# Transposing the state's weights on VectorE in place of TensorE, with later reads and loads, in a fused attention and gated feed-forward kernel

## Chip, cores, metric

One core of one Trainium2 chip. The metric is device time in microseconds, the median of several executions. A profile comes from one execution of the kernel; that of the kernel before took 791.23 us and is not among the three timed ones in the table below. "PE" is TensorE, "DVE" VectorE, "ACT" ScalarE, "POOL" GpSimd, "SP" the engine that issues most DMAs.

## The reference, cut to what matters

```python
# x (8, 8, 512, 64), state (8, 8, 32, 64): batches, heads, tokens, width
scores  = scale * x @ state^T   ; a  = softmax(scores)  ; xread = a  @ state
scores2 = scale * state @ x^T   ; a2 = softmax(scores2) ; sread = a2 @ x
y = concat([xread, sread], axis=2) -> rows of 512        # (4352, 512)
h = y @ w_in                      # 512 -> 2048
out = (h * cos(h)) @ w_out        # 2048 -> 512
```

`a2 @ x` sums over tokens, so TensorE needs a2 with tokens on partitions. The kernel has it with the state rows on partitions (`z2`) and must transpose it: `a2T`. This transpose is what the change moves.

## The kernel before: what the change and the argument touch

```python
class Attention:                       # one for each batch b; ... cuts
    self.spread, self.z2 = xT[:, 0:2], xT[:, 2:4]
    self.a2T = xT[:, 0:2].rearrange("p j (c m) -> p j c m", c=NC)

    def tokens_turned(self, k):        # x, loaded by DMA, turned in 32x32 blocks on DVE (L298)
        blocks = self.xT[:, k].rearrange("p (g i) -> p g i", i=32)
        nc.vector.transpose(out=blocks, in_=blocks)
    def scores(self):                  # PE, L316: needs all four k of xT
        self.per_head(stT, lambda rows, k: self.xT[rows, k, :])
    def norm1(self):                   # DVE, L383: two SBUF inputs
        nc.vector.tensor_tensor(self.aT, self.z1, self.spread, op=ALU.mult)
    def turn(self, j):                 # PE, L389: four transposes of 128x128
        for c in range(NC):
            nc.tensor.transpose(out=at[j][:, P * c:P * c + P],
                                in_=self.z2[:, j, P * c:P * c + P], identity=ident)
    def turn_kept(self, j):            # ACT, L394
        nc.scalar.copy(self.a2T[:, j].rearrange("p c m -> p (c m)"), at[j])
    def reads(self, j):                # PE, L406: weights are a2T, moving operand x_b
        ...
def part(b, name, *args):              # after reads(1) the next loads of x are issued
    ...
def hidden(t):                         # PE, L469: two matmuls, h in one of 2 PSUM buffers
    ...
def gate(t):  ...                      # ACT L475, DVE L478, ACT L483 and L484, DVE L490
# one step: hidden; attention on PE (pe[s]); ACT L475, x_act[s]; DVE L478, x_dve[s];
#           ACT L483, L484; DVE L490; y_act[s], y_dve[s]; then the products of the tile
#           three steps back (L534: two or four matmuls), which sum up in PSUM banks
#           that DVE and ACT copy out (L540, L545, L547: `held`)
def plan(b):                           # which attention part of batch b+1 stands in which step
    ...
    def late(b, s):
        pairs(s[0], b, "turn", "turn_kept", 0)
        pe[s[1]].append((b, "reads", 0))
        pe[s[2]].append((b, "reads", 1))
        x_dve[s[2]].append((b, "keep"))
        if len(s) > 3:
            turned(b, s[3])
    ...
        prod(0, b, 1, *[MAIN for _ in bank])
        prod(4, b, 2, *bank)
        prod(9, b, 3, *bank)
        if b + 1 < B:
            prod(14, b + 1, 0)
            early(b + 1, (1 + (b == 1), 2 + (b == 1), 5, 6, 7, 8, 9))
            late(b + 1, (10, 11, 12, 15))
```

`early(b, s)` takes the steps of: token turns of k = 0, 1; of k = 2, 3; scores; spread and shift; the exponentials; sums; norm1. The "steps of even batches" are those while an even batch b runs.

## Time and profile before

| | before |
|---|---|
| time, median (lowest to highest), 3 runs | 791.73 us (791.41 to 792.08) |
| span of the profiled run | 789.4 us |
| PE, DVE, ACT busy | 97%, 55%, 49% |
| PE idle from 160 to 700 us | two gaps of 0.71 us |

PE at 97% says that time can be won from PE's own work; the two gaps say where it can't. The prediction below shows the lines.

### The profile page before, as it was taken

To read this page: it belongs to the slowest core of one execution; us is meant where nothing else is said; L and a number is where in the kernel's file an instruction comes from. 1 tells how busy PE (TensorE), PEld (TensorE's weight loads), DVE (VectorE), ACT (ScalarE), POOL (GpSimd) and SP (SyncE) were. 2 spreads that over 40 slices of the span, in tenths; PEclk is the share of its full clock that TensorE was granted. 3 is DMA by queue.
4 is the path that set the end of the run, shared out by engine and by line. 5 is a ranking of instruction groups with operands and counts; after the bars stand their busy time and mean duration, and the time that the engine had idled before them with its cause. 6 is when DMAs were issued, how large, how long until landed. Compare 5 with 4: busy or idle time off the path is not lost.

```text
span 789.4 us, 7555 instructions
## 1 busy us (share of the span) xinstructions
PE 767.3 (97%) x2664; PEld 340.4 (43%) x2664; DVE 431.2 (55%) x675; ACT 389.3 (49%) x626; POOL 178.7 (23%) x119
## 2 busy tenths in 40 slices
PE   8998999899999999999999999999999999999997
PEld 3442333344344344444444434434444444455554
DVE  5879887732564467744554467635553545431531
ACT  3877964644364445643473446443563445322222
POOL 3343359684000000551000000740000004610200
PEclk9999999999999999999999999999999999999999
DMA  8485461051010610150003410340100114000021
GB/s 239 160 248 179 127 140 28 0 90 18 0 27 14 107 27 14 30 104 0 15 14 54 80 27 7 53 75 0 27 1 0 27 27 117 17 0 15 14 41 40
DMA packets 161957, 43.49 MB, mean 55 GB/s; under 512 B 153920, under 2 KB 153920, under 8 KB 161920
## 3 DMA queue, kind: packets, MB, share of 16 engines
q1 hardware_dynamic: 161024, 42.49, 24.7%
q10 hardware_dynamic: 768, 0.39, 0.2%
q8 instruction: 21, 0.34, 0.2%
q0 software_dynamic: 128, 0.13, 0.1%
q14 instruction: 16, 0.13, 0.1%
HBM read 34.08 MB, written 8.91 MB: 54 GB/s over the span
## 4 chain that ended last, share of the span: by engine, by line
PE 80%; ACT 9%; DVE 8%; issue 1%; DMA 1%; POOL 1%; SPq 0%; DVEq 0%; POOLq 0%
PE o L534 44%; PE h L469 26%; PE at L316 4%; PE o L654 3%; PE at L406 2%; DVE q L478 1%; ACT q L483 1%; ACT q L484 1%; DVE g_all L490 1%; ACT s L227 1%; ACT q L475 1%; DVE xT L336 1%; ACT xT L362 1%; DVE aT L383 1%; PE o L316 1%
## 5 line engine op out<-in xcount | busy, mean ns | idle before, releaser
L469 PE MATMUL h<-aT,sw 128*128 128x512 f32 x512 | 243.2, 598 | 10.8 <-DVE g_all L490 10.2
L534 PE MATMUL o<-g_all,w_out 128*128 128x512 f32 x512 | 236.4, 598 | 1.1 <-POOL w_out L241 1.1
L496 POOL TENSOR_TENSOR g_all<-g_all 128x512 f32<-128x512 f32 x80 | 112.1, 1424 | 450.8 <-DVE g_all L490 447.2
L475 ACT ACTIVATE q<-h 128x512 f32<-128x512 f32 (+1 forms) x144 | 82.2, 571 | 261.7 <-PE h L469 261.6
L478 DVE SCALAR_TENSOR_TENSOR q<-q,h 128x512 f32<-128x512 f32 (+1 forms) x144 | 94.2, 654 | 207.3 <-ACT q L475 207.3
L534 PE MATMUL o<-g_all,s 128*128 128x512 f32 x384 | 177.3, 598 | 0.0
L490 DVE TENSOR_TENSOR g_all<-h,q 128x512 f32<-128x512 f32 (+1 forms) x144 | 94.8, 658 | 123.9 <-ACT q L484 117.7
L469 PEld LDWEIGHTS h<-aT,sw 128*128 128x128 f32 x512 | 96.8, 191 | 136.2 <-issue 110.2
L534 PEld LDWEIGHTS o<-g_all,w_out 128*128 128x128 f32 x512 | 94.0, 190 | 125.5 <-issue 118.4
L483 ACT ACTIVATE q<-q 128x512 f32<-128x512 f32 (+1 forms) x144 | 87.6, 608 | 96.3 <-DVE q L478 96.3
L534 PEld LDWEIGHTS o<-g_all,s 128*128 128x128 f32 x384 | 70.9, 190 | 91.7 <-issue 87.3
L484 ACT ACTIVATE q<-q,halfpi 128x512 f32<-128x512 f32 (+1 forms) x144 | 100.5, 698 | 4.5
L241 POOL TENSOR_TENSOR w_out<-w_out,s 128x1024 int32<-128x1024 int32 x10 | 23.9, 2389 | 79.4 <-DVE w_out L236 79.4
L496 DVE TENSOR_TENSOR g_all<-g_all 128x512 f32<-128x512 f32 x48 | 33.2, 692 | 1.6
L443 ACT COPY sw<-at 128x512 f32<-128x512 f32 x50 | 26.8, 589 | 9.0 <-PE at L316 9.0
L469 PE MATMUL h<-sT,w_in 128*128 128x256 f32 x128 | 30.2, 379 | 0.0
L654 PE MATMUL o<-w_out,g_all 128*128 128x512 f32 x64 | 29.6, 592 | 0.0
L469 PEld LDWEIGHTS h<-sT,w_in 128*128 128x128 f32 x128 | 24.3, 190 | 10.1 <-issue 6.2
L316 PE MATMUL at<-w_in,stT 64*32 64x512 f32 x400 | 27.2, 601 | 0.0
L241 POOL TENSOR_TENSOR w_in<-w_in,s 128x1024 int32<-128x1024 int32 (+1 forms) x10 | 19.7, 1966 | 32.1 <-DVE w_in L236 18.6
L540 DVE SCALAR_TENSOR_TENSOR held<-o,held 128x512 f32<-128x512 f32 x40 | 25.3, 676 | 2.3 <-PE o L534 2.3
L561 DVE STREAM_TRANSPOSE ot<-held 128x512 f32<-128x512 f32 x32 | 22.2, 692 | 0.0
(83 smaller groups left out, 443.5 us busy)
## 6 DMA issues: line engine op xcount, KB each, us to landing
out_dram<-ot SPq DMA_DIRECT2D x132, 64.0 KB, 2.0
g_all<-in_moe_w_out_dram SPq DMA_DIRECT2D x8, 1024.0 KB, 4.9
g_all<-in_moe_w_in_dram SPq DMA_DIRECT2D x6, 1024.0 KB, 5.2
xT<-in_x_dram SPq DMA_DIRECT2D x96, 64.0 KB, 2.3
x_b<-in_x_dram SPq DMA_DIRECT2D x24, 256.0 KB, 4.7
x_b<-in_x_dram SPq DMA_DIRECT2D x16, 128.0 KB, 3.9
g_all<-in_moe_w_in_dram SPq DMA_DIRECT2D x4, 512.0 KB, 6.0
x_b<-in_moe_w_out_dram SPq DMA_DIRECT2D x1, 1024.0 KB, 6.1
```

What stands on the lines that cost most here:

```text
L241: nc.gpsimd.tensor_tensor(bits, bits, e.bitcast(I32), op=ALU.add)
L316: nc.tensor.matmul(out=(to or at)[j][Ns * k:Ns * k + Ns, 0:n], lhsT=w[D * j:D * j + D, self.b, Ns * k:Ns * k + Ns], rhs=r(slice(D * j, D * ...
L443: (copy or nc.scalar.copy)(sw_of[self.b, nt][:, j, c0:c1], to[j][:, 0:c1 - c0])
L469: nc.tensor.matmul(out=t.hp, lhsT=t.lhs(i), rhs=t.rhs(i), start=(i == 0), stop=(i == t.kn - 1))
L475: nc.scalar.activation(t.q, t.hp, func=ACTF.Copy, bias=MAGIC)
L478: nc.vector.scalar_tensor_tensor(out=t.q, in0=t.q, scalar=MAGIC, in1=t.hp, op0=ALU.subtract, op1=ALU.subtract)
L483: nc.scalar.activation(t.q, t.q, func=ACTF.Abs)
L484: nc.scalar.activation(t.q, t.q, func=ACTF.Sin, bias=halfpi, scale=-TWO_PI)
L490: nc.vector.tensor_tensor(t.g, t.hp, t.q, op=ALU.mult)
L496: engine.tensor_tensor(out, a, b, op=ALU.subtract)
L534: nc.tensor.matmul(out=acc[bank][ch], lhsT=w[:, i, P * ch:P * ch + P], rhs=g.g, start=(i == 0), stop=(i == NH - 1))
L654: nc.tensor.matmul(out=acc[MAIN][i], lhsT=t.g[:, P * i:P * i + P], rhs=w_out[:, :, t.f, :], start=(t.n_th == 0), stop=(t.n_th == NF - 1))
```

## The change

Its intent: take 48 transposes off the busiest engine and give them, as 16 pieces of 32 partitions a batch, to DVE; place the pieces behind norm1 (they overwrite `spread`), so that reads of a2T and the loads that follow must come later, across the end of the batch where the next is even.

```diff
+        def turn_block(self, k, q):
+            src = self.z2.rearrange("p j (c q i) -> p q (j c) i", q=P // 32, i=32)
+            dst = self.a2T.rearrange("p j c m -> p (j c) m")
+            rows = slice(Ns * k, Ns * k + Ns)
+            nc.vector.transpose(out=dst[32 * q:32 * q + 32, :, rows],
+                                in_=src[rows, q])
 ...
+            if b < 2:
+                pairs(s[0], b, "turn", "turn_kept", 0)
 ...
+        def blocks_turned(b, to):
+            for i in range(16):
+                to[i * 5 // 16].append((b, "turn_block", i % NK, i // NK))
 ...
+            elif odd:
+                prod(0, b, 1)
+                turned(b, 1)
+            else:
+                late(b, (None, None, 0))
+                prod(2, b, 1)
+                turned(b, 3)
             prod(4, b, 2, *bank)
-            prod(9, b, 3, *bank)
-            if b + 1 < B:
-                prod(14, b + 1, 0)
-                early(b + 1, (1 + (b == 1), 2 + (b == 1), 5, 6, 7, 8, 9))
-                late(b + 1, (10, 11, 12, 15))
+            prod(9 if odd else 10, b, 3, *bank)
+            if b + 1 < B and odd:
+                prod(13, b + 1, 0)
+                early(b + 1, (2, 3, 5, 6, 7, 8, 9))
+                blocks_turned(b + 1, (x_dve[12], y_dve[12], x_dve[13],
+                                      y_dve[13], x_dve[14]))
+                pe[15].append((b + 1, "reads", 0))
+            elif b + 1 < B:
+                early(b + 1, (4, 5, 6, 7, 8, 9, 10))
+                blocks_turned(b + 1, (y_dve[10], x_dve[11], y_dve[11],
+                                      x_dve[12], y_dve[12]))
+                late(b + 1, (None, 13, 14))
+                prod(15, b + 1, 0)
```

More of the change, by code (lines that the diff above doesn't have):

```diff
@@ L395, in turn_kept @@
                            at[j])
+        def turn_block(self, k, q):
+            src = self.z2.rearrange("p j (c q i) -> p q (j c) i", q=P // 32,
+                                    i=32)
+            dst = self.a2T.rearrange("p j c m -> p (j c) m")
+            rows = slice(Ns * k, Ns * k + Ns)
+            nc.vector.transpose(out=dst[32 * q:32 * q + 32, :, rows],
+                                in_=src[rows, q])
         def reads(self, j):
@@ L781, in late @@
         def late(b, s):
-            pairs(s[0], b, "turn", "turn_kept", 0)
-            pe[s[1]].append((b, "reads", 0))
+            if b < 2:
+                pairs(s[0], b, "turn", "turn_kept", 0)
+            if s[1] is not None:
+                pe[s[1]].append((b, "reads", 0))
             pe[s[2]].append((b, "reads", 1))
@@ L804, in plan @@
         else:
+            odd = b % 2
             bank = (SIDE,) if b == 1 else ()
@@ L807, in plan @@
                 turned(1, 0)
-            prod(0, b, 1, *[MAIN for _ in bank])
-            prod(4, b, 2, *bank)
-            prod(9, b, 3, *bank)
-            if b + 1 < B:
-                prod(14, b + 1, 0)
-                early(b + 1, (1 + (b == 1), 2 + (b == 1), 5, 6, 7, 8, 9))
-                late(b + 1, (10, 11, 12, 15))
+                prod(0, b, 1, MAIN)
+            elif odd:
[5 more added lines that the diff above has]
+                turned(b, 3)
+            prod(4, b, 2, *bank)
+            prod(9 if odd else 10, b, 3, *bank)
[11 more added lines that the diff above has]
+                prod(15, b + 1, 0)
         return pe, x_act, y_act, x_dve, y_dve
```

## The prediction

> **Words.** The feed-forward part is cut in steps: each makes one tile of h (two matmuls, L469), which a gate of five instructions on ACT and DVE turns into g_all; sixteen steps make a batch, numbered 0 to 15. During batch b TensorE also does the attention of batch b+1. "Even" and "odd" mean the running batch b. There are two buffers of h, so the h of step n can't start before the last gate instruction (L490) of step n-2 has ended.
>
> **What bounds the kernel now.** I read the page first, then the groups by form, then the timelines of PE and DVE around the operations that the change touches. From the page, busy time and the chain that ended last:
>
> ```profile
> PE 767.3 (97%) x2664; PEld 340.4 (43%) x2664; DVE 431.2 (55%) x675; ACT 389.3 (49%) x626; POOL 178.7 (23%) x119
> PE 80%; ACT 9%; DVE 8%; issue 1%; DMA 1%; POOL 1%; SPq 0%; DVEq 0%; POOLq 0%
> ```
>
> TensorE is busy for 97% of the span and makes 80% of the chain. The table of stretches puts nearly all of its 22 us of idle time before 160 us and at the very end; from 160 to 700 us its timeline shows two idle gaps, 0.71 us each. So after the start, work taken off TensorE is time, except where TensorE waits anyway. The groups of the pieces that are removed, and of the nearest kin of what is added:
>
> ```profile
> L389 PE MATMUL at<-ident,xT 128*128 128x128 f32 x64 | 8.3, 273 | 0.0
> L394 ACT COPY xT<-at 128x512 f32<-128x512 f32 x16 | 9.2, 576 | 1.4 <-PE o L534 1.4
> L298 DVE STREAM_TRANSPOSE xT<-xT 128x512 f32<-128x512 f32 x24 | 16.9, 703 | 0.0
> ```
>
> 273 ns is the latency of one transpose, not its cost: the group's busy time is 8.3 us for 64. The PE timeline shows the cost; first an even batch (2), then an odd one (3), step 10 of each:
>
> ```profile
> 240.26 1.04 PE L389 MATMUL at<-ident,xT 128*128 128x128 f32 x8
> 241.13 3.60 PE L534 MATMUL o<-g_all,w_out 128*128 128x512 f32 x8
> ```
>
> ```profile
> 321.88 1.88 PE L469 MATMUL h<-aT,sw 128*128 128x512 f32 x4
> 323.59 1.04 PE L389 MATMUL at<-ident,xT 128*128 128x128 f32 x8
> 324.46 1.88 PE L534 MATMUL o<-g_all,s 128*128 128x512 f32 x4
> 327.06 1.98 PE L469 MATMUL h<-aT,sw 128*128 128x512 f32 x4 [0.71 <-DVE g_all L490]
> ```
>
> From start to start eight transposes take 0.87 us (240.26 to 241.13). In the even batch the work around them is gapless. In the odd batch TensorE, just after them, stands still 0.71 us until DVE has ended a gate. DVE there:
>
> ```profile
> 322.27 1.24 DVE L336 STREAM_TRANSPOSE xT<-i 128x1024 f32<-128x1024 f32 x1
> 323.43 0.65 DVE L478 SCALAR_TENSOR_TENSOR q<-q,h 128x512 f32<-128x512 f32 x1
> 324.00 1.80 DVE L383 TENSOR_TENSOR aT<-aT,xT 128x1024 f32<-128x1024 f32 x1
> 325.73 0.70 DVE L561 STREAM_TRANSPOSE ot<-held 128x512 f32<-128x512 f32 x1
> 326.36 0.65 DVE L490 TENSOR_TENSOR g_all<-h,q 128x512 f32<-128x512 f32 x1
> ```
>
> It runs without a gap from 320.93 to 327.01, when L490 of step 9 ends and h of step 11 starts. That queue goes back to the exponentials of step 7 on ACT (table load at 313.31, second load at 318.88); the transposes have no part in it. Batch 5 repeats it (0.71 us at 498.12), batch 1 has 0.98 us at 155.99.
>
> **What the Trainium skill says.** "TensorE: Matmul & The Clock Gate", Part 4 (PE-mode transpose): about 275 ns each within a kernel, and the result lands in PSUM, so that a copy must follow. The trace agrees: 273 ns, and L394 is that copy; but in a row they cost 109 ns each. "VectorE: DVE Perf Modes", The three transpose paths: the DVE transposes blocks of 32x32 only. This is why the change needs 16 pieces, each reading 32 partitions and writing another 32. "VectorE: DVE Perf Modes", The TRN2 errata, gives a fixed cost per instruction, so small pieces pay more per element; the trace has 703 ns for 512 elements and 1236 for 1024, that is about 170 ns fixed. "SBUF — State Buffer", SBUF: two separate sides: VectorE instructions with two SBUF inputs, or in a two-port mode, and those of GpSimd exclude each other. The trace agrees: L383 took 1.21 us at 238.29 with POOL idle and 1.80 us at 324.00 with POOL busy, while the transpose L336 took 1.23 and 1.24 us in the same places. So the pieces should not suffer from POOL.
>
> **The change, part by part.**
> (1) Removed: 6 sets of 8 transposes on PE, 0.88 us each (step 10 lasts 6.03 us in batch 2, without them it would be the usual 5.15). The three of even batches lie on the path: -2.64 us. The three of odd batches stand ahead of a wait whose end DVE sets; without them TensorE waits 0.7 + 0.9 = about 1.6 us instead: 0. Twelve copies on ACT (12 x 0.576 = 6.9 us) also go; ACT is at 49% and they are not in the DVE queue above: 0.
> (2) Added: 96 pieces of 32x256 on DVE. From the line through 703 and 1236 ns, 170 + 256 x 1.04 = 436 ns, and instructions in a row overlap by some 0.08 us: about 0.36 to 0.40 us each, 6 us a batch, 36 us in all. The order lists show 4,3,3,3,3 of them, each set after the first or last gate instruction of a step. A step's gate leaves DVE free about 1.45 us between its two instructions while ACT works, which holds three pieces. In odd batches (steps 12 to 14, of 5.15 and 6.37 us) DVE has about 2 us of other work a step and 2.6 us of pieces: it fits, and h of step n has over 2 us of slack there. In even batches the last three pieces come in the second slot of step 12, and reads of step 13 need all 16. Adding up the queue from step 10 (four pieces, the held copy L547, gate, pieces, gate), I get the last piece ending 6.7 us after h of step 12 begins, and reads due at 5.15 + 1.72 + 0.1 = 6.95. Close: I take 0.1 us of waiting a batch, +0.3.
> (3) Moved: scores, reads, products and keep2 move to other steps, in equal numbers: 0. Reads follow later, loads of x too; about 20 us remain until the tokens are needed, and in the SP timeline 20 loads take about 11 us to issue and 2 to 5 us to land: 0.
> (4) The move that costs. In even batches tokens_turned moves to steps 4 and 5 and scores to step 6, with no step between as before (1, 2 and 5). The last turn is on DVE behind L490 of step 5. How such a slot lies, batch 4 step 2 (h starts at 368.20), DVE:
>
> ```profile
> 371.35 0.70 DVE L298 STREAM_TRANSPOSE xT<-xT 128x512 f32<-128x512 f32 x1
> 372.94 0.69 DVE L490 TENSOR_TENSOR g_all<-h,q 128x512 f32<-128x512 f32 x1 [0.89 <-issue]
> 373.55 0.70 DVE L298 STREAM_TRANSPOSE xT<-xT 128x512 f32<-128x512 f32 x1
> ```
>
> It ends 374.25 - 368.20 = 6.05 us after h of its step began. And step 5, on PE, is a short one:
>
> ```profile
> 384.87 1.88 PE L469 MATMUL h<-aT,sw 128*128 128x512 f32 x4
> 386.68 1.09 PE L316 MATMUL at<-xT,stT 64*32 64x512 f32 x16
> 387.69 1.98 PE L534 MATMUL o<-g_all,w_out 128*128 128x512 f32 x4
> 389.51 1.88 PE L469 MATMUL h<-aT,sw 128*128 128x512 f32 x4
> ```
>
> It lasts 4.64 us with scores (L316, 1.21 with its edges), so 3.43 without. TensorE is ready for scores 3.43 + 1.72 + 0.09 = 5.24 us after h of step 5 began, and their last quarter waits for 6.05 + 0.05. The order list confirms both orders. That is 0.85 us of new waiting; a little of it is hidden, since the other quarters run first: 0.83 x 3 batches = +2.5 us.
> Sum: 791.73 - 2.64 + 0.3 + 2.5 = 791.9. I say 791.8.
>
> **Rivals.** *A, TensorE bound throughout:* all six sets count, -5.3, perhaps -6: 786. For it speaks 97% busy; against it the gap that ends at 327.06. *B, the even half alone:* as mine without (4), because the turn ends earlier or TensorE has slack: 789.1. Against it speaks the measured 6.05. *C, DVE becomes the bound:* pieces cost 0.6 us or more, because they cross partitions or wait for POOL; then a batch adds 10 us of DVE in 13, gates come late and reads wait 1 to 2 us each: 796 to 800. For it: no such form is in the trace. Against it: L336 beside POOL, and L416 with 32 partitions at 0.29 us. *D, reads in step 13 wait 0.5 us or more:* 793.
>
> **Range and chances.** Mine with (2) between 0 and 0.4 us a batch gives 791.6 to 792.8; B's side gives 789; so 789.6 to 793.2, with A at about 5% and C at about 4% outside. 2% would be 15.8 us, three times all the TensorE work that goes: faster 0.01, same 0.97, slower 0.02.
>
> **What would show it.** Right: no L389 in batches for 2 to 7; in even batches h of step 10 to 11 shorter by 0.9 us, but a new PE gap of about 0.8 us at scores of step 6, released by DVE xT; in odd batches the 0.71 us gap before h of step 11 grown to about 1.6 us; pieces of 0.36 to 0.44 us. Wrong if the scores start without a gap, if the odd gap stays at 0.7 us or less, or if pieces take over 0.5 us.

## The result

The changed kernel takes **794.82 us** (794.62 to 795.47, 6 runs) against 791.76 (791.35 to 792.12, 6 runs) of the kernel before in the same rounds. The ratio is 1.004, 95% interval 1.0027 to 1.0053: slower, clear of the noise, and well within 2%. A ratio is the mean time of one kernel's fast runs over that of the other's fast runs of the same rounds, so it is not quite the ratio of the medians. The change costs 3 us where I expected none: the size of the effect lies outside the predicted range.

The changed kernel's line numbers are 10 higher from L406 on (L406 is now L416, L469 is L479, L534 is L544, L490 is L500, L547 is L557); L389, L394 and all before them keep theirs, and the pieces are L404. So L416 on PE, in the kernel after, is reads; L416 on DVE, in the kernel before, is `keep`. First the page of the profile after, busy times, chain, and the group of the pieces (there count, busy us, mean ns):

```profile
PE 767.6 (97%) x2616; PEld 336.2 (42%) x2616; DVE 472.6 (60%) x771; ACT 383.2 (48%) x614; POOL 178.5 (23%) x119
PE 69%; DVE 13%; ACT 13%; issue 2%; DMA 1%; POOL 1%; SPq 0%; ACTq 0%; DVEq 0%; POOLq 0%
L404 DVE STREAM_TRANSPOSE xT<-xT 32x256 f32<-32x256 f32 x96 | 41.8, 436 | 1.8
```

PE runs 48 matmuls fewer and yet counts as busy for as long (767.6 against 767.3 us): the record of one matmul runs on after the next has started (at scores a record lasts 0.59 to 0.61 us, and in the kernel before sixteen of them start within 0.50 us), so a short wait hides under the records ahead of it. So idle time of PE is not the place to look; the distance between the starts of h is. That is also how the chain tells it: PE's share fell from 80 to 69%, and DVE and ACT, whose ends PE now waits for, rose from 17 to 26%.

To find the places I took, from PE's timeline, the start of h in each step (L469, L479). One long stretch holds all six sets: from h of step 7 in batch 1 to h of step 7 in batch 7. It takes 649.56 - 136.89 = 512.67 us before and 653.39 - 137.33 = 516.06 after: **+3.39 us**. (The start of the program, up to h of that first step 7, differs between the profiles by up to 1.2 us, which this stretch leaves out; it is a sharper measure than the time, and the table of experiments uses it. It is one execution of each kernel, though, so a dip of the granted clock inside it has to be looked for.) Step by step it differs from the predicted plan in four places.

**Scores, even batches, step 6.** PE of the kernel after, batch 4 (columns: start, length, engine, line, operation, tiles, shapes, count; an fp32 matmul counts twice in these profiles, so the two of h are x4, while a transpose counts once):

```profile
390.02 1.88 PE L479 MATMUL h<-aT,sw 128*128 128x512 f32 x4
391.83 2.00 PE L316 MATMUL at<-xT,stT 64*32 64x512 f32 x16
393.76 3.70 PE L544 MATMUL o<-g_all,w_out 128*128 128x512 f32 x8
```

Scores take 391.83 to 393.76 = 1.93 us where they took 1.02 before. No idle is shown: twelve of the 16 records start by 392.32, the last four only from 392.71 on, and the earlier records cover the time between. They wait for DVE's token turn of the last k:

```profile
391.35 0.69 DVE L500 TENSOR_TENSOR g_all<-h,q 128x512 f32<-128x512 f32 x1 [0.31 <-ACT q L494]
391.95 0.70 DVE L298 STREAM_TRANSPOSE xT<-xT 128x512 f32<-128x512 f32 x1
```

It ends at 392.65, 6.06 us after h of step 5 (386.59). I had said 6.05. The step costs 0.90 us more than its work: 7.27 against 5.15 + 1.22.

**Reads, even batches, step 13.** PE, then the queue of DVE from step 10 on, batch 4:

```profile
427.86 1.88 PE L479 MATMUL h<-aT,sw 128*128 128x512 f32 x4
429.67 0.43 PE L416 MATMUL at<-x_b,xT 128*64 128x128 f32 x2
430.30 1.09 PE L416 MATMUL at<-x_b,xT 128*64 128x128 f32 x14 [0.20 <-DVE xT L404]
431.31 1.98 PE L544 MATMUL o<-g_all,w_out 128*128 128x512 f32 x4
```

```profile
419.35 1.76 DVE L404 STREAM_TRANSPOSE xT<-xT 32x256 f32<-32x256 f32 x4
421.05 0.64 DVE L557 TENSOR_SCALAR held<-o 128x512 f32<-128x512 f32 x1
421.72 0.69 DVE L488 SCALAR_TENSOR_TENSOR q<-q,h 128x512 f32<-128x512 f32 x1
422.44 1.33 DVE L404 STREAM_TRANSPOSE xT<-xT 32x256 f32<-32x256 f32 x3
423.93 0.69 DVE L500 TENSOR_TENSOR g_all<-h,q 128x512 f32<-128x512 f32 x1 [0.16 <-ACT q L494]
424.65 1.34 DVE L404 STREAM_TRANSPOSE xT<-xT 32x256 f32<-32x256 f32 x3
426.02 0.69 DVE L488 SCALAR_TENSOR_TENSOR q<-q,h 128x512 f32<-128x512 f32 x1
426.74 1.34 DVE L404 STREAM_TRANSPOSE xT<-xT 32x256 f32<-32x256 f32 x3
428.16 0.69 DVE L500 TENSOR_TENSOR g_all<-h,q 128x512 f32<-128x512 f32 x1
428.86 1.38 DVE L404 STREAM_TRANSPOSE xT<-xT 32x256 f32<-32x256 f32 x3
```

Three pieces take 1.34 us: 0.44 each, and they do not overlap. Of the 96 pieces only the first of each batch starts before the instruction ahead of it has ended (by 0.08 us); it alone reads and writes from partition 0 on, as the 128-partition instruction ahead does. The other 90 start 0.01 us or more after that end. The trace before had shown the same on 32-partition instructions in a row, the four of L416, each at another partition:

```profile
336.69 1.18 DVE L416 TENSOR_TENSOR sr<-at,i 32x128 f32<-32x128 f32 x4
```

Their mean is 0.285 us, and 4 x 0.285 = 1.14: no overlap there either. That the partition decides is read from these places; no run tests it. From 418.74 to 430.24 us DVE stands still for more than 0.03 us only twice (0.16 and 0.08 us), so what each piece is longer than I took adds up through the queue. The last ends at 430.24, 7.53 us after h of step 12 (422.71); I had said 6.7. Reads are due at 429.67, two of their matmuls do start, and the other 14 go on at 430.30: 0.63 us lost, of which the profile calls 0.20 idle.

**The bank of step 11, odd batches.** PE of the kernel after, batch 3:

```profile
323.11 1.88 PE L479 MATMUL h<-aT,sw 128*128 128x512 f32 x4
324.83 1.88 PE L544 MATMUL o<-g_all,s 128*128 128x512 f32 x4
328.28 1.98 PE L479 MATMUL h<-aT,sw 128*128 128x512 f32 x4 [1.57 <-DVE g_all L500]
330.10 2.74 PE L544 MATMUL o<-g_all,s 128*128 128x512 f32 x6
333.07 1.13 PE L544 MATMUL o<-g_all,s 128*128 128x512 f32 x2 [0.23 <-DVE held L557]
334.04 1.88 PE L479 MATMUL h<-aT,sw 128*128 128x512 f32 x4
```

and the kernel before, same place:

```profile
328.97 1.09 PE L406 MATMUL at<-x_b,xT 128*64 128x128 f32 x16
329.99 3.70 PE L534 MATMUL o<-g_all,s 128*128 128x512 f32 x8
```

The gap ahead of h of step 11 has grown from 0.71 to 1.57 us, as foretold: here the removal is worth nothing. But then the products want a PSUM bank whose sum of the last phase DVE has not yet copied out (L557). Before, reads stood between h and these products and gave DVE that time. They have moved away, and the wait they had covered is open: the step takes 5.75 us where its work is 5.26, so 0.49 us in batches 3 and 5.

**The bank of step 11, even batches.** The same copy, L557, stands behind four pieces (419.35 to 421.05 above). The step takes 5.32 in place of 5.15 us: 0.17 (in e5 and e6 below, which take the pieces away from there, it is gone).

The sum: even batches 3 x (-0.88 + 0.90 + 0.63 + 0.17) = +2.46, odd ones 2 x 0.49 = +0.98, together +3.44 us against 3.39 measured in the stretch.

### The profile page after: what moved, and what is told of

Read it like the earlier page. It is cut to its first block, busy times and chain, and to the rows that moved or that the text cites. A ratio compares the mean times of both kernels' runs of the same rounds, so it can differ in the third digit from the quotient of the medians.

```text
span 793.1 us, 7552 instructions
## 1 busy us (share of the span) xinstructions
PE 767.6 (97%) x2616; PEld 336.2 (42%) x2616; DVE 472.6 (60%) x771; ACT 383.2 (48%) x614; POOL 178.5 (23%) x119
## 4 chain that ended last, share of the span: by engine, by line
PE 69%; DVE 13%; ACT 13%; issue 2%; DMA 1%; POOL 1%; SPq 0%; ACTq 0%; DVEq 0%; POOLq 0%
PE o L544 37%; PE h L479 22%; PE at L316 4%; PE o L664 3%; DVE q L488 3%; ACT q L493 3%; ACT q L494 3%; DVE g_all L500 2%; DVE xT L404 2%; PE at L416 2%; ACT xT L362 1%; ACT q L485 1%; DVE xT L336 1%; ACT L494 1%; ACT aT L357 1%
## 5 line engine op out<-in xcount | busy, mean ns | idle before, releaser
L479 PE MATMUL h<-aT,sw 128*128 128x512 f32 x512 | 242.5, 596 | 13.3 <-DVE g_all L500 12.8
L544 PE MATMUL o<-g_all,w_out 128*128 128x512 f32 x512 | 236.9, 599 | 1.2 <-POOL w_out L241 1.2
L544 PE MATMUL o<-g_all,s 128*128 128x512 f32 x384 | 177.8, 598 | 0.5 <-DVE held L557 0.5
L500 DVE TENSOR_TENSOR g_all<-h,q 128x512 f32<-128x512 f32 (+1 forms) x144 | 94.8, 659 | 103.0 <-ACT q L494 99.5
L479 PEld LDWEIGHTS h<-aT,sw 128*128 128x128 f32 x512 | 96.4, 190 | 138.2 <-issue 111.4
L544 PEld LDWEIGHTS o<-g_all,w_out 128*128 128x128 f32 x512 | 93.8, 190 | 127.7 <-issue 121.1
L544 PEld LDWEIGHTS o<-g_all,s 128*128 128x128 f32 x384 | 71.1, 190 | 94.9 <-issue 87.9
L404 DVE STREAM_TRANSPOSE xT<-xT 32x256 f32<-32x256 f32 x96 | 41.8, 436 | 1.8
L479 PE MATMUL h<-sT,w_in 128*128 128x256 f32 x128 | 30.2, 379 | 0.0
L479 PEld LDWEIGHTS h<-sT,w_in 128*128 128x128 f32 x128 | 24.3, 190 | 10.1 <-issue 6.2
```

The source lines that it names most:

```text
L404: nc.vector.transpose(out=dst[32 * q:32 * q + 32, :, rows], in_=src[rows, q])
L479: nc.tensor.matmul(out=t.hp, lhsT=t.lhs(i), rhs=t.rhs(i), start=(i == 0), stop=(i == t.kn - 1))
L500: nc.vector.tensor_tensor(t.g, t.hp, t.q, op=ALU.mult)
L544: nc.tensor.matmul(out=acc[bank][ch], lhsT=w[:, i, P * ch:P * ch + P], rhs=g.g, start=(i == 0), stop=(i == NH - 1))
```

## The experiments

All are edits of the changed kernel, five timed rounds each. "Stretch" is the one defined above (512.67 before, 516.06 after). "Over before" is the difference of medians to the kernel before in the same call; runs of one call share a chip.

| run | median us | over before | stretch us | stretch, against |
|---|---|---|---|---|
| changed kernel | 794.82 | +3.06 | 516.06 | +3.39, before |
| e1 tokens earlier | 792.35 | +1.09 | 513.40 | -2.66, changed |
| e2 reads later | 793.02 | +1.76 | 514.22 | -1.84, changed |
| e3 products at 11 | 794.50 | +3.24 | 515.06 | -1.00, changed |
| e4 odd turns on PE | 795.00 | +3.74 | 516.53 | +0.47, changed |
| e5 even turns on PE | 795.43 | +3.90 | 516.74 | +0.68, changed |
| e6 all three | 789.30 | -2.23 | 510.04 | -6.02, changed |
| e7 odd sooner | 789.07 | -2.46 | 510.34 | +0.30, e6 |
| e8 e7, odd turns on PE | 792.15 | +0.62 | 513.48 | +3.14, e7 |
| e9 stores later | 787.72 | -4.11 | 508.81 | -1.23, e6 |
| e10 norm1 later (again) | 785.78 (785.68) | -6.05 (-5.83) | 506.79 (again) | -3.25, e6 |
| e11 e9 and e10 | 786.07 | -5.76 | 506.80 | +0.01, e10 |
| e12 wrong result | 791.52 | -0.31 | not used | |
| e13 e10, all turns on PE | 790.70 | -0.81 | 512.04 | +5.25, e10 |

The 95% interval of a ratio is about 0.13% (1 us) either way, so differences under 1 us are read from the stretch, not from the time. The first profiled execution of e10 had a granted clock of 0.994 against 0.998 of its repeat and a stretch of 508.06: its clock was halved for 3.4 us from 152.1 us on, inside the stretch. I use the repeat. The profile of e4 has such a dip too (see there); the stretch of no other run has one.

### e1: the token turns one step earlier

```diff
-                early(b + 1, (4, 5, 6, 7, 8, 9, 10))
+                early(b + 1, (3, 4, 6, 7, 8, 9, 10))
```

> Edit: in even batches the tokens are turned in steps 3 and 4 in place of 4 and 5; scores stay in step 6. Theory (three named waits: scores of step 6 wait 0.9 us for the last token turn in each of three even batches): the step from h of step 6 to h of step 7 falls from 7.27 to 6.37 us, in all 3 x 0.9 = 2.7 us less than the changed kernel, 792.1 us. Rival (DVE is loaded with the pieces and gates come late everywhere; where a token turn stands doesn't matter): within 0.5 us of the changed kernel, 794.8 us.

The stretch fell by 2.66 us and the median is 792.35. Scores in batch 4, PE:

```profile
390.69 1.09 PE L316 MATMUL at<-xT,stT 64*32 64x512 f32 x16
391.71 3.70 PE L544 MATMUL o<-g_all,w_out 128*128 128x512 f32 x8
```

1.02 us again. The pieces are where they were, so DVE's load is not the cause of this part: the order is.

### e2: reads behind the pieces

```diff
-                late(b + 1, (None, 13, 14))
-                prod(15, b + 1, 0)
+                late(b + 1, (None, 14, 15))
+                prod(13, b + 1, 0)
```

> Edit: in even batches reads move from steps 13 and 14 to 14 and 15, and the next batch's first products from 15 to 13. Theory (reads of step 13 wait for the last three pieces): step 13 falls from 5.28 to 4.65 us, 3 x 0.63 = 1.9 us less than the changed kernel, 792.9 us. Rival (the loads of x, which follow reads, become late by another step): a new wait of tokens for a DMA in odd batches, 795 us or more.

Step 13 fell to 4.65 us in each even batch and the stretch by 1.84. No new wait for the tokens' DMAs appeared; the loads of x, though another step later, are hidden still.

### e3: products in the step that reads left

```diff
-                prod(13, b + 1, 0)
+                prod(11, b + 1, 0)
                 early(b + 1, (2, 3, 5, 6, 7, 8, 9))
```

> Edit: in odd batches the next batch's first products move from step 13 to step 11. Theory (with reads gone from step 11, the product of step 11 meets a PSUM bank that DVE has not yet copied out, L557): the products fill that wait; step 11 plus step 13 of batches 3 and 5 fall together by 0.49 us, 2 x 0.49 = 1.0 us less than the changed kernel, 793.8 us. Rival (the copy is late because of the whole DVE queue, and moves with it): the wait stays, 794.8 us.

The stretch fell by 1.00. Steps 11 and 13 of batch 3 take 6.47 + 5.15 = 11.62 us against 5.75 + 6.37 = 12.12, and no wait for `held` is left in PE's timeline. The median, 0.3 us under the changed kernel's, does not resolve this by itself.

### e4: the odd batches' transposes back on PE

```diff
-                blocks_turned(b + 1, (x_dve[12], y_dve[12], x_dve[13],
-                                      y_dve[13], x_dve[14]))
+                pairs(10, b + 1, "turn", "turn_kept", 0)
```

> Edit: in odd batches the transposes go back to TensorE in step 10, as before the change, with its copies on ACT; everything else as in the changed kernel. 24 transposes on PE come back, 48 pieces leave DVE. Theory (in odd batches TensorE waits in step 10 to 11 for a gate of DVE anyway, so the transposes there are free): 794.8 us, within 0.4 of the changed kernel, and the gap before h of step 11 falls from 1.57 to about 0.7 us. Rival A (TensorE bound throughout): 3 x 0.88 = 2.6 us more, 797.4 us. Rival B (the pieces' load on DVE costs time in odd batches): 793.5 us or less.

24 transposes came back, and the stretch grew by 0.47 us, not by 2.6. All of it is in batch 1, where steps 10 and 11 take 11.26 us against 10.80; from h of step 7 in batch 3 to that in batch 5 it takes 172.38 against 172.37 us. Batch 3, PE:

```profile
324.90 1.04 PE L389 MATMUL at<-ident,xT 128*128 128x128 f32 x8
325.77 1.88 PE L544 MATMUL o<-g_all,s 128*128 128x512 f32 x4
328.36 1.98 PE L479 MATMUL h<-aT,sw 128*128 128x512 f32 x4 [0.70 <-DVE g_all L500]
```

The gap is 0.70 us again in place of 1.57. In batches 3 and 5 the transposes were free, as step (1) of the prediction said. Batch 1 can't tell: in this execution the granted clock was 0.50 from 150.9 to 154.3 us, in step 10 of batch 1:

```profile
150.48 3.39 PE L479 MATMUL h<-aT,sw 128*128 128x512 f32 x4 [1.86 <-DVE g_all L500]
153.67 1.36 PE L389 MATMUL at<-ident,xT 128*128 128x128 f32 x8
```

This h takes 3.39 us where it took 1.98 in the changed kernel, the transposes 1.36 in place of 1.04. By estimate 3.4 us at half the clock are up to 1.7 us of lost work, more than the 0.98 us that PE stood still there in the kernel before; so the 0.47 us are put down to the dip. The profile of e8 below has none: step 10 of batch 1 takes 5.55 us there, with the transposes, as in e7 without them.

### e5: the even batches' transposes back on PE

```diff
-                blocks_turned(b + 1, (y_dve[10], x_dve[11], y_dve[11],
-                                      x_dve[12], y_dve[12]))
+                pairs(11, b + 1, "turn", "turn_kept", 0)
```

> Edit: in even batches the transposes go back to TensorE (step 11, after norm1 of step 10), with their copies on ACT; everything else as in the changed kernel. Theory (in even batches the removed transposes were worth 0.88 us each, and the pieces cost 0.63 us at reads of step 13 and 0.17 us at the bank of step 11): 3 x (0.88 - 0.80) = 0.2 us more than the changed kernel, 795.0 us; the scores' wait of 0.9 us stays. Rival (the pieces' load on DVE is what makes the even batches longer): 2 us less or more, 792.8 us.

+0.68 us: 0.11 and 0.10 from batch 1 to 3 and from 3 to 5, as expected, and 0.47 from batch 5 to 7. Of the last, 0.35 lies in one place, step 6 of batch 6 (7.62 in place of 7.27 us), where L500 of step 5 starts 0.34 us later behind ACT; why is open. The rival is out: with 48 pieces fewer on DVE the steps 11 and 13 of even batches lost just the 0.17 and 0.63 us of waiting, step 11 gained the transposes' 0.88, and no other step became shorter.

### e6: the three together

The edits of e1, e2 and e3, and the even pieces half a step later, behind the copy L557:

```diff
-                blocks_turned(b + 1, (y_dve[10], x_dve[11], y_dve[11],
-                                      x_dve[12], y_dve[12]))
+                blocks_turned(b + 1, (x_dve[11], y_dve[11], x_dve[12],
+                                      y_dve[12], x_dve[13]))
```

> Edit: e1, e2 and e3 together, and the even batches' pieces begin half a step later (first slot of step 11 to first slot of step 13), behind the copy L557 in place of ahead of it. Theory: the three waits and the 0.17 us add up, 794.8 - 2.7 - 1.9 - 1.0 - 0.5 = 788.7 us; that is 3 x 0.88 = 2.6 us under the kernel before, which is the even batches' share of the transposes, with 0.4 us to spare. Rival (waits taken away come back elsewhere): not under 790.5 us.

-6.02 us of stretch where the parts were to give 6.1, and 789.30 us: ratio 0.9967 (0.9954 to 0.9979), faster than the kernel before by 0.3%. The four waits account for the whole loss, and the even half of the removal comes out: 512.67 - 510.04 = 2.63 = 3 x 0.88.

### e7 and e8: the odd batches one step sooner

The waits ahead of h of step 11 in odd batches were left (1.59 us in batch 3 of e6). I held them for latency that starts with the exponentials.

```diff
-            prod(4, b, 2, *bank)
+            prod(3 if odd and b > 1 else 4, b, 2, *bank)
...
-                early(b + 1, (2, 3, 5, 6, 7, 8, 9))
+                early(b + 1, (2, 3, 5, 6, 7, 8, 9) if b == 1
+                      else (2, 3, 4, 5, 6, 7, 8))
```

> Edit: e6, and in batches 3 and 5 everything from scores to norm1 stands one step earlier (scores in step 4, the exponentials in step 6), with the third products in step 3. Theory (the wait before h of step 11 is the end of the chain that the exponentials of step 7 set off, ahead of three short steps; one step earlier it has a long step more): the two waits of 1.57 us go, 788.7 - 3.1 = 785.6 us. Rival (DVE's load in steps 7 to 10 sets the end whatever the order): within 0.7 us of e6, 788.7 us.

**That theory fell.** The stretch is e6's within 0.3 us. The wait moved to h of steps 9 and 10 (0.37 and 1.06 us). DVE ahead of the second, e7, batch 3:

```profile
318.70 1.25 DVE L550 SCALAR_TENSOR_TENSOR held<-o,held 128x512 f32<-128x512 f32 x2
319.87 0.67 DVE L488 SCALAR_TENSOR_TENSOR q<-q,h 128x512 f32<-128x512 f32 x1
320.46 1.21 DVE L383 TENSOR_TENSOR aT<-aT,xT 128x1024 f32<-128x1024 f32 x1
321.59 0.70 DVE L571 STREAM_TRANSPOSE ot<-held 128x512 f32<-128x512 f32 x1
322.22 0.65 DVE L500 TENSOR_TENSOR g_all<-h,q 128x512 f32<-128x512 f32 x1
```

DVE has no gap here. What binds, then, is the amount of DVE work in three short steps, ahead of the gate's last instruction; e9 and e10 test that.

> Edit: e7, with the transposes of odd batches back on TensorE in step 10. Theory (there is no wait left in batches 3 and 5 that would hide them, batch 1 still has one): 2 x 0.88 = 1.8 us more than e7, 787.4 us, while in e4 the same edit cost nothing. Rival (the transposes of odd batches are hidden in any case): as e7.

e8 puts the odd transposes back into e7. It costs 3.14 us: 1.29 in each of batches 3 and 5, 0.56 in batch 1. The same edit as in e4, which cost nothing in batches 3 and 5 there; here h of step 11 waits only 0.1 us, and nothing hides them. It is more than the 0.87 that the transposes take, since step 11 grows as well (6.40 to 6.82): its moved products wait for ACT's second copy of the transposes (L394, which ends at 330.40 us) out of the same PSUM bank, and go on at 330.45. The 0.56 us of batch 1 are in step 11 too (6.47 to 7.03), and step 10 there, with its wait, still hides the transposes.

### e9, e10, e11: taking DVE work out of that queue

e9 holds two output transposes back; e10 moves norm1 by one step; e11 does both. All on top of e6.

```diff
# e9
-        if later:
+        if later and not (t.b in (3, 5) and s in (8, 9, 10)):
             later.pop(0)()
# e10
-                early(b + 1, (2, 3, 5, 6, 7, 8, 9))
+                early(b + 1, (2, 3, 5, 6, 7, 8, 10))
```

> Edit: e6, and in batches 3 and 5 the two output transposes (the L561 of the kernel before) leave steps 8 and 9 and follow from step 11 on. e7 showed that one step more of latency doesn't help. Theory now (the wait before h of step 11 is DVE's queue behind gate L478 of step 9: norm1 1.8 us, one output transpose 0.63 us, then L490): without the output transpose L490 comes 0.63 us sooner: 2 x 0.63 = 1.3 us less than e6, 788.0 us. Rival (the end is set by ACT's second activation, not by DVE's queue): as e6, 789.3 us.

-1.23 us; the wait ahead of h of step 11 is 0.97 in place of 1.59 us.

> Edit: e6, and in odd batches (1 too) norm1, 1.8 to 2.1 us on DVE beside a busy POOL, moves from step 9 to step 10, behind the gate of step 9. Theory (DVE's queue sets that wait): batch 1 gains about 1.85 us, its whole wait; batches 3 and 5 about 0.8 us each, until ACT's activation of step 9 sets the end: 3.4 us less than e6, 785.9 us. Rival (norm1 only moves the wait to h of step 12): as e6, 789.3 us.

-3.25 us, and 785.78 us, ratio 0.9926 (0.9914 to 0.9939). DVE in batch 3 (the repeat of e10); the gate's last instruction, L500, now follows an idle DVE and waits for ACT:

```profile
321.23 0.65 DVE L488 SCALAR_TENSOR_TENSOR q<-q,h 128x512 f32<-128x512 f32 x1
321.81 0.69 DVE L571 STREAM_TRANSPOSE ot<-held 128x512 f32<-128x512 f32 x1
323.33 0.69 DVE L500 TENSOR_TENSOR g_all<-h,q 128x512 f32<-128x512 f32 x1 [0.83 <-ACT q L494]
324.06 0.69 DVE L506 TENSOR_TENSOR g_all<-g_all 128x512 f32<-128x512 f32 x1
324.67 0.68 DVE L488 SCALAR_TENSOR_TENSOR q<-q,h 128x512 f32<-128x512 f32 x1
325.26 1.70 DVE L383 TENSOR_TENSOR aT<-aT,xT 128x1024 f32<-128x1024 f32 x1
```

> Edit: e9 and e10 together. Theory: with norm1 gone ACT sets the end in batches 3 and 5, so the output transposes no longer matter: as e10, 785.9 us. Rival (DVE's queue still sets it): another 0.6 to 1.2 us less, 785.0 us.

As e10 (506.80 and 506.79): with norm1 gone ACT sets the end and the output transposes no longer matter. This confirms the second theory from both sides.

### e12 and e13: what the removal is worth without the waits

> Edit: e10 with all six sets of transposes back on TensorE (step 11), none on DVE. What the change is worth where the waits around it are gone. Theory (each set now lies on TensorE's path): 6 x 0.88 = 5.3 us more than e10, 791.2 us. Rival (DVE's freedom from 36 us of pieces gives back as much): as e10.

e12 gave a wrong result, by an error of mine: in odd batches I put the transposes into step 11, where the moved products are, and they overwrote the PSUM bank before it was copied out. Its time is not used. e13 has them in step 12:

```diff
# on top of e10; odd, then even
-                blocks_turned(b + 1, (x_dve[12], ... x_dve[14]))
+                pairs(12, b + 1, "turn", "turn_kept", 0)
-                blocks_turned(b + 1, (x_dve[11], ... x_dve[13]))
+                pairs(11, b + 1, "turn", "turn_kept", 0)
```

> Edit: e12 mended: e10 with all six sets of transposes back on TensorE, in step 12 of odd batches and step 11 of even ones, none on DVE. Theory (each set lies on TensorE's path now): 6 x 0.88 = 5.3 us more than e10, 791.1 us. Rival (DVE's freedom from the pieces gives back as much): as e10, 785.8 us.

> e10 once more, beside e13 on the same chip: 785.8 us by its first run.

790.70 against 785.68 us on the same chip: 5.0 us, and 5.25 of stretch, which is 6 x 0.875. So the transfer from PE to DVE is worth all of its PE time once nothing on PE waits for the pieces and nothing else hides the transposes. The rearranged order alone, without the pieces (e13), is worth 0.6 us of stretch against the kernel before (512.04 against 512.67); the times do not resolve it (ratio 0.9991, 0.9978 to 1.0005).

## Why the prediction was wrong, point by point

- **Direction.** "Within 2%" was right, and that the removal would not come out was right. The size was not: I said 791.8 in 789.6 to 793.2, and it is 794.82.
- **Step (1), the removed transposes: right.** 0.88 us in even batches (e5, e6, e13), 0 in odd batches 3 and 5 (e4; the gap grew from 0.71 to 1.57 us, and I said about 1.6). Rival A is out. But my account of that gap, a chain from the exponentials of step 7, was incomplete: e7 shifted it and won nothing, e10 shortened DVE's queue and did.
- **Step (4), scores: right.** 0.90 us against 0.83, x 3 = 0.2 of the miss. The profile shows it as longer scores, not as the gap I had announced.
- **Step (2), the even pieces ahead of reads: this term failed by size.** I took 0.1 us a batch and it is 0.63. The length of a piece, 436 ns, was right. But I had subtracted an overlap of some 0.08 us that I had seen between 128-partition instructions; the pieces follow each other at 0.44 to 0.47 us, and L416 in the trace before could have told me. The queue from step 10 to 12 is all but full, so the excess of 16 pieces arrives at the end whole. I also had the reads' margin at a quarter of a microsecond, and wrote "close". 3 x 0.53 = 1.6 us of the miss. Rival D (0.5 us or more) was right in this. The odd half of the step was right: steps 12 to 14 there take 5.15, 6.37 and 5.15 us, with no wait.
- **Step (3), "moved ... in equal numbers: 0": this step failed.** I counted the moved work, and not what it had been covering. Reads in step 11 of odd batches had hidden PE's wait for a bank: 2 x 0.49 = 1.0 us. e3 shows it by putting other work there. In even batches the pieces moved ahead of the copy of the same kind: 3 x 0.17 = 0.5 us, which I had in the queue as L547 but did not follow to its reader. The step's other half held: no step waits for the later loads of x.
- Together 0.2 + 1.6 + 1.0 + 0.5 = 3.3 us. Added to my sum of 791.9 that is 795.2, against 794.82 measured.
- **Rival C, DVE as the bound throughout: out.** It needed 0.6 us or more for a piece, and they take 0.44 beside a busy POOL as well; and taking 48 of them away (e5) shortened nothing but the two waits already named.

## What to carry to other kernels

When work moves off the busiest engine, list for each moved item what waited behind it and what it was covering: here a wait laid bare made 1.0 of the 3.3 us. Work removed just ahead of a wait that another engine ends is worth nothing until that wait is gone; put it down to the amount of queued work or to latency by moving one instruction of the queue, not by argument. And where a queue is full from end to end, take an instruction's length, and whether it overlaps the next, from a form that is like it in its partitions too: small errors add up at its end, where the reader stands.

## What the Trainium skill lacked or had wrong

- "VectorE: DVE Perf Modes", The three transpose paths, compares single transposes. The page doesn't give what a row costs: here eight 128x128 fp32 transposes on PE cost 0.87 us in a row, and the same data as 16 pieces 16 x 0.436 = 7.0 us on DVE.
- The same page has a length for fp32 `tensor_tensor`, but for a transpose only that of one 128x128 bf16. The runs show fp32 transposes of 436, 703 and 1236 ns for 256, 512 and 1024 elements a partition, and the 32-partition piece is no cheaper than this line says.
- "SBUF — State Buffer", SBUF: two separate sides, says what excludes GpSimd but doesn't name the transpose. Here it is not affected: 422 to 442 ns in all 96 pieces, with a mean of 435 in the 36 that had POOL busy and 436 in the others, while norm1 took 1.21 us beside an idle and 1.79 beside a busy POOL, as the page says of two SBUF inputs.
- No page that I read says that a wait between matmuls can hide under the records of those ahead and be counted as busy: scores took 1.93 in place of 1.02 us with no idle shown, and reads lost 0.63 us with 0.20 shown.
